# Sliding-window attention and a two-layer MoE block on one core: batch 1 in groups of three steps, another order of the first loads, and more idle matmuls ahead of the first MoE unit

## The chip, the cores and the metric

The kernel runs on one core of a Trainium2 chip. The core has a matrix engine (TensorE, PE in the profile; its weight loads are PEld), VectorE (DVE), ScalarE (ACT), GpSimd (POOL) and SyncE (SP). Each engine works through its own list of instructions in the order in which the program gives them, and waits where a semaphore says so. Data come from the device memory by DMA; here GpSimd issues nearly all loads. The metric is the device time of one execution in microseconds (us), lower is better. It is given as a median of several runs.

## The reference

Eight batches of eight heads, 576 tokens, head width 64. Each token sees the tokens at a distance of at most 32. The result is put together to 4608 rows of 512 and goes through two dense layers with a squared ReLU between them.

```python
scores = scale * np.matmul(q, k.transpose(0, 1, 3, 2))
mask = np.abs(pos[:, None] - pos[None, :]) <= window          # window = 32
scores = np.where(mask, scores, -1000000000.0)
attn = np.exp(scores - max); attn = attn / (sum(attn) + 1e-09)
x = np.matmul(attn, v)      # (8, 8, 576, 64), then transposed and reshaped to (4608, 512)
h = x @ w_in                # (512, 2048)
r = np.maximum(h, 0.0)
out = (r * r) @ w_out       # (2048, 512)
```

## The kernel before

**Steps and tiles.** The attention goes in steps of 64 tokens ("chunks"), nine for a batch, 72 in all, numbered n = 9 b + c. The MoE block goes in nine tiles T of 512 tokens, that is, of eight chunks, so that a tile does not end where a batch ends: tile 1 is chunks 8 to 15, and chunk 8 is the last of batch 0.

**Loading.** The tokens of a batch come in five or six pieces of at most 128 tokens (L37 to L39). `kBX`, `qBX` and `vBX` in the list `ORDER` (L33) are piece X of batch B; `w1D` and `w2D` are quarters of the two weights. `ORDER` is the order in which GpSimd issues these loads at the start (L459, L524, L541, L546). K and Q of batches 0 and 1 are turned by PE (`tok_turn`, L464: transposes at L482, then copies out of PSUM by VectorE and, in batch 0, ScalarE). From batch 2 on a transposing DMA on SyncE does this (`dma_turn`, L512). Loads from batch 2 on also wait for a certain MoE unit (`pace`, L501).

**Attention.** Batches 0 and 1 go in groups of one or two chunks, from batch 2 on in groups of three; `FB = 2` (L26) sets the border, and `build` (L882) takes the one path or the other. For a group of two, `scores` (L560) makes 16 small matmuls, ScalarE an exp (L598), VectorE one masked product for each chunk (L607); `av` (L694) then makes eight matmuls a chunk, `evac` (L717) divides by the row sums on VectorE (L722, L724), and `xturn` (L731) transposes on PE and copies with ScalarE into `XT`, the input of the first MoE layer. For a group of three, the middle chunk uses a copy of K with its halves in another order (`ka`, L586). The masked products (L613, L619) lay the three chunks out so that `av3` (L628) needs two times eight matmuls for all three; its results are copied out of PSUM (`evac3`, L645: L655 by VectorE, L652 by ScalarE), added (L657), and divided (L659, L662). `xturn3` (L668) turns the result, by DMA for n of at least `NPE` = 18, else on PE through bank D. In the code of before only chunks from 18 on reach it, so its PE part isn't used. PSUM has eight banks: A, C, B, D for the attention, two for the first layer (`HT`), two for the second (`OUTP`).

**MoE.** `mm1` and its variants for 128 tokens (`mm1_small`, L749) and 256 (`mm1_half`, L771) are the first layer; a unit of any of them is followed by a ReLU on ScalarE and a square on VectorE. Tile 0 and the first half of tile 1 have small units, the second half of tile 1 and tile 2 half ones. A small unit (g, q) of tile 0 needs token group g (chunks 2 g and 2 g + 1) and quarter q of the first weight. `mm2` (L837) is the second layer: unit x is 128 tokens and has four segments of four matmuls, one for each quarter of the second weight. Units take turns in the two `OUTP` banks; units 2 and 3 lie in banks B and D.

**What sets the order.** Each operation is recorded with its engine, what it reads and writes, a key and an estimated duration (`rec`, L61). `schedule` (L264) plays the program forward with these durations and a model of the load queue, works backward from the end to get due times, repeats this with several margins, and keeps the order per engine that has the shortest modelled end. That order is then fixed. A change of keys, banks or load order therefore can move operations of all engines.

**Idle matmuls.** `fill` (L305) puts matmuls on zeros (L408, 128 columns, into the second `OUTP` bank) into the planned gaps of PE, up to 36 us, but not beyond the transposes of piece 3 of batch 0 (`idle_end`, L490). In a gap that begins before 8 us (planned) the number is 1.15 times the gap over 107 ns, later 0.5 times the gap over 54 ns:

```python
for k in range(int((gap - 60) * (DENSE if at < COLD else SPARSE) // one)):
```

Of the kernel before, what the change touches and what calls it, by code (L numbers as in the profile page):

```python
# [8 lines left out]
BF16 = mybir.dt.bfloat16  # L9
# [13 lines left out]
WARM, COLD, DENSE, SPARSE = 36000, 8000, 1.15, 0.5  # L23
NPE = 18
TOFF, TST = 6, 0.9
# [7 lines left out]
ORDER = ("k01 q01 v00 v01 k02 q02 v02 w10 k03 q03 v03 w11 k04 q04 v04 w12 w13 w20 w21 w22 w23 k05 q05 "  # L33
         "k10 q10 v10 k11 q11 v11 k12 q12 v12 k13 q13 v13 k14 q14 v14").split()
# [12 lines left out]
class Prog:  # L47
# [310 lines left out]
class Gen:  # L358
# [82 lines left out]
    def pieces(self, b):  # L441
        return PIECE2 if b >= FB else PIECE if b else PIECE0
# [21 lines left out]
    def tok_turn(self, b, x, key):  # L464
# [95 lines left out]
    def scores(self, n, m):  # L560
# [23 lines left out]
        if m > 2:  # L584
# [4 lines left out]
                reads=self.qk_tags(b, c + 1) + [("sc", n - 3)], writes=[("ka", i, ki)], key=key - 1, dur=300, att=True)  # L589
# [78 lines left out]
    def xturn3(self, n, y):  # L668
# [10 lines left out]

        def f(e):  # L680
            for w, np in ((0, 128), (1, 64)):
                for t in range(4):
                    mm = e.transpose(bass.AP(self.TRP, 0, [[1024, 128], [1, 1]]) if False else self.TRP[:, 512 * w + np * t:512 * w + np * t + np],
                                     self.XR[0:np, 2 * y + w, 128 * t:128 * t + 128], self.ID[0:np, 0:np])
            return mm

        self.p.rec("PE", f, reads=[("xr", 2 * y), ("xr", 2 * y + 1), "id"], writes=["sD"], key=key, dur=340, att=True)
        for w, np in ((0, 128), (1, 64)):
            t0 = 64 * (n + 2 * w)
            src = self.TRP[:, 512 * w:512 * w + 4 * np].rearrange("p (f q) -> p f q", f=4)  # L690
            self.p.rec("ACT", lambda e, a=src, t0=t0, np=np: e.activation(self.XT[:, :, t0:t0 + np], a, ACTF.Copy), reads=["sD"],
# [57 lines left out]
    def mm1_small(self, T, g, q, key):  # L749
# [6 lines left out]
        def f(e):  # L756
            for d in range(4 * q, 4 * q + 4):
                for ft in range(4):
# [78 lines left out]
    def mm2(self, T, u, seg, key):  # L837
# [5 lines left out]
        if x in (2, 3):  # L843
            tag = "sB" if x == 2 else "sD"
            op = self.BK[tag[1]]
# [36 lines left out]
    def build(self):  # L882
# [18 lines left out]
        for b in range(B_):  # L901
# [23 lines left out]
            for c in range(NCH):  # L925
                n = NCH * b + c
                if b >= FB:
                    if c % 3 == 0:
                        self.scores(n, 3)
# [5 lines left out]
                        self.evac3(n, y)  # L935
                        self.xturn3(n, y)
                    continue
                m = 1 if not c or n in (1, 8) else 2
                if n not in self.group:
# [7 lines left out]
                    if n + m < FB * NCH and n + m != 8:  # L947
# [59 lines left out]
```

## Time and profile before

| what | value |
|---|---|
| median of 4 runs | 304.28 us (302.97 to 306.46) |
| the profiled execution: its own time | 305.64 us |
| its span, first to last instruction | 303.8 us |
| mean granted TensorE clock | 0.994 |
| busy: PE, DVE, ACT, POOL | 291.4, 173.4, 157.1, 106.6 us |
| GpSimd's load queue (q0) | 18.16 MB |
| first MoE unit starts | 15.80 us |

The page of the profile describes one execution. Busy times are the union of an engine's instructions. "40 slices" cuts the span into equal parts and gives each engine's busy share in tenths; PEclk is the clock that TensorE was granted, in tenths of full speed. The timeline lists an engine's instructions in order: start, duration, engine, line, operation, output and inputs, count, and in brackets the idle time before it and what ended that. A matmul's duration includes the time until its result has come out, so where matmuls follow each other closely their spacing, not their duration, says what each costs. In the view of DMA issues the last number is the time from issue to landing.

### The profile page before, as it was taken

The numbers are of one execution on the slowest core, as the hardware profiler recorded it, in microseconds if no ns is written. First come the engines' busy times: TensorE is split into PE (matmuls) and PEld (weight loads), VectorE is DVE, ScalarE is ACT, GpSimd is POOL, SyncE is SP. The second block draws the span as 40 slices with busy tenths as digits, with TensorE's granted clock in tenths as the row PEclk, the third lists the DMA queues.
The fourth block names the chain that finished last, engine by engine and source line by source line (L and its number), as shares of the span: only waits on it lengthen the run. The fifth ranks groups of instructions, "written<-read, shape, count | busy, mean of one in ns | idle before, by whom it ended". The sixth has DMA issues, their size and how long they took to land.

```text
span 303.8 us, 6966 instructions
## 1 busy us (share of the span) xinstructions
PE 291.4 (96%) x2726; PEld 171.3 (56%) x2763; DVE 173.4 (57%) x427; ACT 157.1 (52%) x261; POOL 106.6 (35%) x133
## 2 busy tenths in 40 slices
PE   8577999999999999999999999999999999999996
PEld 7477955886758764444454445454445444444444
DVE  6546424775698995668565795677457732222200
ACT  3345622745748763665465665555645644344411
POOL 8999374142415540552054534334320000000000
PEclk9979999999999999999999999999999999999999
DMA  9999999999999999999799999999995220000022
GB/s 110 154 186 207 191 155 194 157 175 144 161 121 168 121 131 205 144 112 166 156 127 134 145 155 186 114 160 127 171 126 66 63 60 35 37 35 35 36 95 80
DMA packets 166673, 39.07 MB, mean 129 GB/s; under 512 B 157808, under 2 KB 162160, under 8 KB 166640
## 3 DMA queue, kind: packets, MB, share of 16 engines
q0 software_dynamic: 115200, 18.16, 90.1%
q1 hardware_dynamic: 45472, 10.96, 25.7%
q10 hardware_dynamic: 5968, 9.51, 10.4%
q8 instruction: 22, 0.36, 0.5%
q14 instruction: 11, 0.09, 0.1%
HBM read 36.70 MB, written 9.44 MB: 152 GB/s over the span
## 4 chain that ended last, share of the span: by engine, by line
PE 89%; DVE 3%; DMA 3%; POOL 2%; issue 1%; ACT 1%; DVEq 0%; POOLq 0%
PE outp L849 36%; PE ht L798 27%; PE ht L759 7%; PE ht L780 6%; PE sc L578 3%; DMA w<-in_moe_w_in_dram 3%; PE sc L638 3%; PE sc L849 2%; DVE xr L662 1%; POOL vx L524 1%; PE sc L482 1%; PE sc L712 1%; PE sc L711 1%; PE sc L823 1%; PE outp L823 1%
## 5 line engine op out<-in xcount | busy, mean ns | idle before, releaser
L849 PE MATMUL outp<-w,gt 128*128 128x512 bf16 x506 | 125.8, 379 | 1.4 <-issue 0.3
L813 DVE TENSOR_TENSOR gt<-rt 128x512 bf16<-128x512 bf16 x144 | 59.7, 419 | 67.4 <-ACT rt L804 56.8
L798 PE MATMUL ht<-xt,w 128*128 128x512 bf16 x371 | 94.0, 379 | 1.0 <-issue 0.5
L804 ACT ACTIVATE rt<-ht 128x512 bf16<-128x512 f32 x96 | 57.2, 599 | 59.9 <-PE ht L798 57.0
L849 PEld LDWEIGHTS outp<-w,gt 128*128 128x128 bf16 x528 | 49.8, 98 | 54.6
L798 PEld LDWEIGHTS ht<-xt,w 128*128 128x128 bf16 x384 | 36.3, 98 | 41.7
L459 POOL DMA_DIRECT2D qraw<-in_q_dram x40 | 34.8, 871 | 50.1 <-PE ht L798 26.5
L459 POOL DMA_DIRECT2D kraw<-in_k_dram x40 | 34.9, 872 | 41.6 <-PE ht L798 17.8
L524 POOL DMA_DIRECT2D vx<-in_v_dram x40 | 34.6, 867 | 26.2 <-PE ht L798 12.6
L598 ACT ACTIVATE e<-sc 128x1024 bf16<-128x1024 f32 (+1 forms) x47 | 37.1, 822 | 11.1 <-PE sc L578 11.1
L856 ACT ACTIVATE oe<-outp 128x512 f32<-128x512 f32 x33 | 19.8, 599 | 23.7 <-PE outp L849 23.7
L759 PE MATMUL ht<-xt,w 128*128 128x128 bf16 x384 | 24.3, 223 | 2.8 <-DMA w<-in_moe_w_in_dram 2.1
L759 PEld LDWEIGHTS ht<-xt,w 128*128 128x128 bf16 x384 | 22.5, 100 | 3.6 <-issue 2.2
L662 DVE TENSOR_TENSOR xr<-pf,rs 128x512 bf16<-128x512 f32 (+1 forms) x36 | 23.7, 681 | 0.5 <-DVE ka L586 0.2
L780 PE MATMUL ht<-xt,w 128*128 128x256 bf16 x192 | 23.8, 273 | 0.0
L765 ACT ACTIVATE rt<-ht 128x512 bf16<-128x512 f32 x24 | 14.3, 599 | 16.0 <-PE ht L759 15.9
L780 PEld LDWEIGHTS ht<-xt,w 128*128 128x128 bf16 x192 | 17.9, 98 | 3.2
L786 ACT ACTIVATE rt<-ht 128x512 bf16<-128x512 f32 x24 | 14.3, 602 | 10.1 <-PE ht L780 8.6
L619 DVE TENSOR_TENSOR pt<-e,mask 128x512 bf16<-128x512 bf16 x36 | 15.2, 421 | 5.6 <-ACT e L598 5.5
L655 DVE COPY pf<-sc 128x520 f32<-128x520 f32 x18 | 12.6, 698 | 6.6 <-PE sc L638 6.4
L657 DVE TENSOR_TENSOR pf<-pf 64x520 f32<-64x520 f32 x18 | 12.6, 698 | 5.9 <-ACT pf L652 5.2
L536 DVE COPY vd<-vx 64x528 bf16<-64x528 bf16 (+1 forms) x28 | 12.5, 447 | 5.9 <-PE sc L578 4.6
(80 smaller groups left out, 211.6 us busy)
## 6 DMA issues: line engine op xcount, KB each, us to landing
out_dram<-oe ACTq DMA_DIRECT2D x35, 256.0 KB, 3.2
kraw<-in_k_dram POOLq DMA_DIRECT2D x30, 128.0 KB, 6.1
qraw<-in_q_dram POOLq DMA_DIRECT2D x30, 128.0 KB, 5.3
vx<-in_v_dram POOLq DMA_DIRECT2D x24, 128.0 KB, 5.4
w<-in_moe_w_in_dram POOLq DMA_DIRECT2D x4, 512.0 KB, 11.4
w<-in_moe_w_out_dram POOLq DMA_DIRECT2D x4, 512.0 KB, 18.5
vx<-in_v_dram POOLq DMA_DIRECT2D x16, 96.0 KB, 5.9
xt<-xr SPq DMA_TRANSPOSE x36, 4.2
```

Source lines behind the costliest of these rows:

```text
L459: self.p.rec("POOL", lambda e: e.dma_start(dst, src), writes=[("fraw", b, t, x)], old=[("fraw", b - 2, t, y + (b == 2))], reads=self.pace( ...
L524: self.p.rec("POOL", lambda e: e.dma_start(self.VX[b % 2][r:r + n, s, :, 0:64], self.v[b, :, t0:t0 + n, :].rearrange("h p d -> p h d")), w ...
L598: self.p.rec("ACT", lambda e, d=dst, a=src: e.activation(d, a, ACTF.Exp, scale=0.125), reads=["s" + x for x in name], writes=[("e", h)], k ...
L619: self.p.rec("DVE", lambda e, a=pt, c=ee, d=mb: e.tensor_tensor(a, c, d, ALU.mult), reads=[("e", k // 2), "mask"], writes=[("ptt", k)], ol ...
L662: self.p.rec("DVE", lambda e, w=w, np=np: e.tensor_tensor(bass.AP(self.XR, 512 * (2 * y + w), [[2048, np], [64, 2], [128, 4], [1, 64]]), b ...
L759: mm = e.matmul(ht[:, 128 * (d % 4):128 * (d % 4) + 128], self.W1[:, ft, 128 * d:128 * d + 128], self.XT[:, ft, t0:t0 + 128], start=(ft == ...
L780: mm = e.matmul(ht[:, 256 * (d % 2):256 * (d % 2) + 256], self.W1[:, ft, 128 * d:128 * d + 128], self.XT[:, ft, 64 * s0:64 * s0 + 256], st ...
L798: mm = e.matmul(ht[:], self.W1[:, ft, 128 * d:128 * d + 128], self.XT[:, ft, 512 * T:512 * T + 512], start=(ft == 0), stop=(ft == 3))
L804: self.p.rec("ACT", lambda e: e.activation(rt[:], ht[:], ACTF.Relu), reads=[("ht", k % 2)], writes=[("rt", k % 4)], key=key, dur=560)
L813: self.p.rec("DVE", lambda e: e.tensor_tensor(g, r, r, ALU.mult), reads=[("rt", k % 4)], writes=tags, key=key, dur=430)
L849: mm = e.matmul(op, gt[:, d, 128 * u:128 * u + 128], self.W2[:, d, :], start=(d == 0), stop=(d == 15))
L856: self.p.rec("ACT", lambda e: e.activation(oe[:], op, ACTF.Copy), reads=[tag], writes=[("oe", x % 4)], key=key, dur=560)
```

## The change

- `TB = 1`: batch 1 goes in groups of three chunks, its K and Q in the pieces of the later batches (`PIECE2`). Its pieces are still turned by PE (`TX = 5` sends none to the DMA), through bank D or B in turn, and the results of its groups are turned by PE through bank A instead of D.
- `ORDER`: pieces 4 of batch 0 come ahead of the second quarter of the first weight; piece 5 of batch 0 and pieces 0 and 1 of batch 1 come ahead of the second weight.
- `SPARSE` goes from 0.5 to 0.95, and 16 idle matmuls (`EXTRA`) are put immediately ahead of the first MoE unit, if that is planned ahead of the transposes of piece 3.
- The second layer of tile 0 does its units two by two, through all four segments, in the two `OUTP` banks; banks B and D are not used for it.

```diff
-WARM, COLD, DENSE, SPARSE = 36000, 8000, 1.15, 0.5
+WARM, COLD, DENSE, SPARSE, EXTRA = 36000, 8000, 1.15, 0.95, 16
 NPE = 18
+TB, TX = 1, 5
...
-ORDER = ("k01 q01 v00 v01 k02 q02 v02 w10 k03 q03 v03 w11 k04 q04 v04 w12 w13 w20 w21 w22 w23 k05 q05 "
-         "k10 q10 v10 k11 q11 v11 k12 q12 v12 k13 q13 v13 k14 q14 v14").split()
+ORDER = ("k01 q01 v00 v01 k02 q02 v02 w10 k03 q03 v03 k04 q04 v04 w11 w12 w13 k05 q05 k10 q10 v10 k11 q11 v11 "
+         "w20 w21 w22 w23 k12 q12 v12 k13 q13 v13 k14 q14 v14").split()
...
         for op in sorted((o for o in out if o.eng == "PE"), key=lambda o: o.start):
             gap = min(op.start, WARM, self.idle_end.start) - at
             one = 107 if at < COLD else 54
-            for k in range(int((gap - 60) * (DENSE if at < COLD else SPARSE) // one)):
+            for k in range(int((gap - 60) * (DENSE if at < COLD else SPARSE) // one) + (EXTRA if op is self.first and op.start < self.idle_end.start else 0)):
...
-                w.inc, w.val, w.sem, w.start, w.end, w.dur, w.key = False, None, None, at + one * k, 0, one, -99
+                w.inc, w.val, w.sem, w.start, w.end, w.dur, w.key = False, None, None, min(at + one * k, op.start - 1), 0, one, -99
...
     def pieces(self, b):
-        return PIECE2 if b >= FB else PIECE if b else PIECE0
+        return PIECE2 if b >= TB else PIECE if b else PIECE0
...
-        elif b or x == 5:
+        elif b:
+            u = "DB"[x % 2]
+            ps = self.BK[u].bitcast(BF16)
+            parts = [("k", "s" + u, ps[:, 0:512]), ("q", "s" + u, ps[:, 512:1024])]
+        elif x == 5:
             parts = [("k", "sD", self.TRP[:, 0:512]), ("q", "sD", self.TRP[:, 512:1024])]
...
-                reads=self.qk_tags(b, c + 1) + [("sc", n - 3)], writes=[("ka", i, ki)], key=key - 1, dur=300, att=True)
+                reads=self.qk_tags(b, c + 1) + ([("sc", n - 3)] if b > 1 or c else []), writes=[("ka", i, ki)], key=key - 1, dur=300, att=True)
...
+        trp = self.BK["A"].bitcast(BF16)
+
         def f(e):
             for w, np in ((0, 128), (1, 64)):
                 for t in range(4):
...
-        self.p.rec("PE", f, reads=[("xr", 2 * y), ("xr", 2 * y + 1), "id"], writes=["sD"], key=key, dur=340, att=True)
+        self.p.rec("PE", f, reads=[("xr", 2 * y), ("xr", 2 * y + 1), "id"], writes=["sA"], key=key, dur=340, att=True)
...
-        self.p.rec("PE", f, reads=[("xt", 8 * T + 2 * g), ("xt", 8 * T + 2 * g + 1), ("w1", q)], writes=[("ht", k % 2), ("mo", k)], key=key,
+        first = self.p.rec("PE", f, reads=[("xt", 8 * T + 2 * g), ("xt", 8 * T + 2 * g + 1), ("w1", q)], writes=[("ht", k % 2), ("mo", k)], key=key,
                    dur=900)
+        if not k:
+            self.p.first = first
...
         gt, op, tag = self.GT[T % 2], self.OUTP[x % 2][:], ("outp", x % 2)
-        if x in (2, 3):
-            tag = "sB" if x == 2 else "sD"
-            op = self.BK[tag[1]]
...
-            for seg in range(4):
-                for u in range(4):
-                    self.mm2(0, u, seg, 0.5 + seg + 0.1 * u)
+            for h in range(2):
+                for seg in range(4):
+                    for u in (2 * h, 2 * h + 1):
+                        self.mm2(0, u, seg, 0.5 + 2 * h + 0.5 * seg + 0.1 * (u % 2))
...
             for c in range(NCH):
                 n = NCH * b + c
-                if b >= FB:
+                if b >= TB:
                     if c % 3 == 0:
+                        if b == 1 and not c:
+                            for x in range(2):
+                                self.tok_turn(1, x, n - LEAD - 3)
                         self.scores(n, 3)
...
                         self.evac3(n, y)
+                        if b == 1 and c < 6:
+                            for x in range(2, 4) if not c else (4,):
+                                if x < TX:
+                                    self.tok_turn(1, x, n - LEAD)
+                                else:
+                                    for t in "kq":
+                                        self.dma_turn(1, t, x, n - LEAD)
                         self.xturn3(n, y)
```

More of the change, by code (lines that the diff above doesn't have):

```diff
@@ L682, in f @@
                 for t in range(4):
-                    mm = e.transpose(bass.AP(self.TRP, 0, [[1024, 128], [1, 1]]) if False else self.TRP[:, 512 * w + np * t:512 * w + np * t + np],
-                                     self.XR[0:np, 2 * y + w, 128 * t:128 * t + 128], self.ID[0:np, 0:np])
+                    o = 512 * w + np * t
+                    mm = e.transpose(trp[:, o:o + np], self.XR[0:np, 2 * y + w, 128 * t:128 * t + 128], self.ID[0:np, 0:np])
             return mm
-        self.p.rec("PE", f, reads=[("xr", 2 * y), ("xr", 2 * y + 1), "id"], writes=["sD"], key=key, dur=340, att=True)
+        self.p.rec("PE", f, reads=[("xr", 2 * y), ("xr", 2 * y + 1), "id"], writes=["sA"], key=key, dur=340, att=True)
         for w, np in ((0, 128), (1, 64)):
             t0 = 64 * (n + 2 * w)
-            src = self.TRP[:, 512 * w:512 * w + 4 * np].rearrange("p (f q) -> p f q", f=4)
-            self.p.rec("ACT", lambda e, a=src, t0=t0, np=np: e.activation(self.XT[:, :, t0:t0 + np], a, ACTF.Copy), reads=["sD"],
+            src = trp[:, 512 * w:512 * w + 4 * np].rearrange("p (f q) -> p f q", f=4)
+            self.p.rec("ACT", lambda e, a=src, t0=t0, np=np: e.activation(self.XT[:, :, t0:t0 + np], a, ACTF.Copy), reads=["sA"],
                        writes=[("xt", n + 2 * w + u) for u in range(np // 64)], key=key, dur=200 + 2.8 * np, att=True)
@@ L946, in build @@
                     self.scores(n, m)
-                    if n + m < FB * NCH and n + m != 8:
+                    if n + m < TB * NCH and n + m != 8:
                         bb, cc = divmod(n + m, NCH)
```

## The prediction

> **What bounds the kernel now.** I read the page first, for the engine that is never free and for the slices in which it is.
>
> ```profile
> PE 291.4 (96%) x2726; PEld 171.3 (56%) x2763; DVE 173.4 (57%) x427; ACT 157.1 (52%) x261; POOL 106.6 (35%) x133
> ...
> PE   8577999999999999999999999999999999999996
> ...
> PEclk9979999999999999999999999999999999999999
> ```
>
> A slice is 7.6 us. From the fifth on PE is full; the chain of waits gives PE 89%. So time can be gained only by giving PE less to do, or by filling the first four slices. Idle matmuls (L408) count as busy there, so I added up the spacing of starts in the PE timeline from 15.7 us (first MoE unit) to 28.7: 6 units (L759, 96 matmuls) and the attention of batch 0 would take 8.3 us at full rate (16 matmuls at 56 ns are 0.9 us, six units 5.4; transposes, scores and AV 2.9). The stretch is 13.0 us long. Of the 4.7 us lost, 2.66 is bare idle, 0.41 idle matmuls, and 1.6 slow matmuls and short hand-overs. From 28.7 to the last matmul PE is idle for only 2.5 us in all. The place is the first 29 us.
>
> Next the windows view, cut where the granted clock changes and in equal steps around (columns: stretch, its length, busy PE, PEld, DVE, ACT and POOL with counts, granted clock, DMA share, GB/s):
>
> ```profile
> 8.28:11.70 3.42, 2.39 (x51) 1.87 (x50) 2.85 (x9) 1.07 (x2) 3.42 (x5) 1.00 1.62 144
> 11.70:15.11 3.41, 1.51 (x24) 1.08 (x22) 1.30 (x4) 1.51 (x2) 3.41 (x5) 1.00 1.87 168
> 15.11:18.52 3.41, 2.72 (x30) 2.75 (x31) 0.35 (x2) 0.60 (x1) 3.41 (x6) 0.50 1.63 189
> 18.52:21.94 3.42, 2.31 (x48) 1.91 (x46) 2.67 (x6) 2.11 (x3) 3.42 (x6) 1.00 1.87 180
> ```
>
> After a stretch with PE 44% busy the next one runs at half clock; after 70% and 68% it runs at full clock. Then the PE timeline and the landings:
>
> ```profile
> 13.49 0.19 PE L712 MATMUL sc<-vx,pt 128*128 128x65 bf16 x1
> 15.80 1.86 PE L759 MATMUL ht<-xt,w 128*128 128x128 bf16 x16 [2.12 <-DMA w<-in_moe_w_in_dram]
> ...
> 19.79 0.40 PE L740 MATMUL outp<-identw,xr 128*128 128x128 bf16 x4 [0.76 <-DVE kt L498]
> ...
> 25.86 0.40 PE L740 MATMUL outp<-identw,xr 128*128 128x128 bf16 x4 [1.20 <-DVE kt L498]
> ```
>
> ```profile
> w<-in_moe_w_in_dram POOLq DMA_DIRECT2D x1, 512.0 KB, 10.5
> vx<-in_v_dram POOLq DMA_DIRECT2D x1, 96.0 KB, 10.5
> ```
>
> The first line is w11, issued at 10.44 and landed at 21.0; the second v04, 12.92 to 23.4. Issue plus landing, read so for each load, gives a queue that delivers in order: a 128 KB piece every 0.85 us, a weight quarter every 2.5 us (w12 25.9, w13 28.4, w20 31.0, w23 38.6, k05 38.9). PE's gaps are the 2.12 us for w10 and then the latency of batch 0's attention.
>
> **The new order of loads.** Nothing ahead of w10 moves: w10 stays at 15.7. Then, with the spacings above: k04, q04, v04 land at 19.3, 20.2, 20.9 (2.5 us sooner); w11 at 23.4 (2.4 later); w12 and w13 unchanged; k05, q05, and k10 to v11 from 28.6 to 33.9 (10 sooner); w20 to w23 at 36.4, 38.9, 41.5, 44.1 (5.4 later); k12 to v14 again by 51. On POOL only the order changes: w11 is issued three issues of 0.87 us later, at 13.0 instead of 10.44, still 10 us ahead of its landing, and the loads of batch 2 follow as before.
>
> What PE can do: from 15.7 to 23.4 only w10 is there, so two units (1.8 us; the third token group is not ready) and 2.9 us of attention: up to 3.0 us idle, more than before. But from 23.4 two weight quarters and soon a third meet three or four ready token groups, so I take PE as full: 5.3 us to 28.7. Together 10.0 us against 8.3: **1.65 us gained**, if the clock holds. Next, is the later w2 late? From 23.4 there are 14 units (12.6 us), 1.7 of batch 0's attention, and turns and scores of batch 1 (1.4): PE reaches 39 before it needs w20. Then segments of 1.73 us (8 matmuls, 216 ns) for tokens 0 and 1 end at 40.8, 42.5, 44.2 and 45.9, each after its quarter's landing. Cost nothing; if PE were 3 us earlier it would wait those 3 us, no more.
>
> **Idle matmuls and reserve.** 16 matmuls at 54 to 107 ns are 0.9 to 1.7 us, inside the 2.12 us gap: free. The denser filling adds some 22 to the 25 issued there now (1.2 us) to gaps of that size; where a planned gap doesn't exist they delay work, by 0.3 us at most, as the rows from 8 to 14 us have 1.4 us idle besides the large gap. They lift 1.51 us busy to about 2.9 of 3.41. Here a rule speaks against: the Trainium skill, "TensorE: Matmul & The Clock Gate", section "Why this matters for your kernels", says that no gap under about 3 us costs the clock; by it a gap of 2.12 is harmless and the reserve worth nothing. The row shows half clock after that gap, in a stretch that was 44% busy. By the row the reserve saves about 1.1 of the 1.65 us (16 MoE matmuls at 106 instead of 56 ns, 0.8; AV and transposes 0.3); by the rule nothing. I go with the row. The same page (Part 1) has the activity window free-running, so in some runs it may fall well anyway: this profiled execution took 305.64 us, the four runs 302.97 to 306.46. The sum below is against 305.64 and I carry its difference to the median, 304.28; if half of the runs never had the drop, 0.5 us of it isn't there.
>
> **Batch 1 in threes.** AV goes from 72 matmuls to 48; both kinds are spaced 30 ns in the PE timeline: 0.7 us less. Scores: 24 in 0.46 us (76.53 to 76.99) against 16 in 0.34: 0.2 less. Three hand-overs fewer at about 0.1: 0.3. Transposes of the result, 24 of which 12 are half wide, against 18 whole: nothing. So **1.2 us less on PE**, the bound. VectorE pays, by batch 2's rows:
>
> ```profile
> L655 DVE COPY pf<-sc 128x520 f32<-128x520 f32 x18 | 12.6, 698 | 6.6 <-PE sc L638 6.4
> L657 DVE TENSOR_TENSOR pf<-pf 64x520 f32<-64x520 f32 x18 | 12.6, 698 | 5.9 <-ACT pf L652 5.2
> ```
>
> With the masks (0.42, 0.69, 0.42), the key copy (0.29), the reciprocal (0.25) and two L662 (0.68) a group is 4.8 us, 14.3 for three, against 8 now: 6.3 more, ScalarE about 2 more. Between 40 and 75 us VectorE is busy for 18.6 of 35; the cover is the MoE work that PE has in stock. A new wait comes with bank A: the transposes of a group go there and ScalarE empties it, so the next group's scores wait for the whole group before. PE takes its queue in order: behind those scores stand second-layer segments of tile 0 and small units of tile 1, and ScalarE's Relu and VectorE's squares wait for these. Batch 2 shows 7.6 to 11.3 us from scores to the last L662; with transposes and copies 9 to 12.5. Group 2 can score at 50 (k13 lands at 47.5), group 3 at 59 to 62.5, and chunk 15 is ready at 68 to 75. PE's stock without it: 12.6 + 13.8 (second layer of tile 0) + 7.2 (8 small units of tile 1) + 6.9 (its second layer, tokens 0 and 1) + 8.0 attention = 48.5, to 71.9, or 74 if reckoned from the state of before at 73.6 less what is gained. So 0 to 3 us; I take nothing, as most of the interval lies below. The mm2 banks: token 2 now waits for ScalarE's 0.6 us copy of token 0 while token 1's 0.86 us segment runs: 0 to 0.3, taken as nothing. Attention that starts sooner may close some of the 2.5 us of late gaps, 0 to 1; I take 0.5.
>
> Sum: 305.64 - 1.65 - 1.2 - 0.5 = 302.3 for a profiled execution, and **301.0** for the median.
>
> **Rivals.**
> 1. The early stretch closes almost wholly (0.20): units are placed so that the 3.0 us idle shrinks by 2. Then 299.0. For it: PE works at full rate from 23.4; against: no second quarter earlier.
> 2. The reserve doesn't do what it says (0.12): the planner puts the transpose of k03 ahead of the first unit, so that no reserve is made; or the drop moves one stretch on, where PE has 1.6 of 3.4 us of work. Then the 1.1 us stay lost, and the 0.5 with them: 302.6.
> 3. Slower (0.21): PE runs dry in front of chunk 15. Place: near 72 to 74 us, at the first half-wide unit of tile 1. Each microsecond that chunk 15 is later than 74 is lost. It decides once the loss exceeds the 3.3 gained, at about 77. VectorE at 90% from 80 to 100 us, with the same groups, speaks for it; against it, that even batch 2's slowest group gives 75. With groups 2 and 3 each 4 us above the middle (72), at 80, the time is 307.
>
> **How the numbers follow.** The forecast has 0.47. A measurement of this kernel can tell about 1%, 3 us, from no change. Of the forecast's chance three quarters lie below 301.2, with rival 1's 0.20 that is 0.53 or so faster by over 1%; a quarter, rival 2 and a little of rival 3 give 0.29 within 1%; the rest of rival 3, 0.18, slower. The range goes from rival 1 with its bound, 298.5, to the milder part of rival 3, 306.
>
> **What would show it.** Right: granted clock 1.00 from 5 us on; w11 at 23.4 and w20 at 36.4; seven units by 28.7; PE idle under 3 us from 23.4 on; AV of batch 1 in 48 matmuls. Wrong: a half-clock stretch after 15; PE waiting for w20; an idle PE near 72; idle matmuls that push attention back before 15 us.

## The result, and the profile after

The changed kernel takes **303.39 us** (median of 44 runs, 302.1 to 305.8), the kernel before, run beside it, 304.7 (63 runs). The ratio is 0.9964, with an interval of 0.9953 to 0.9975: 0.36% or 1.1 us faster, which is within 1%, where 301.0 and 1.1% were forecast. Ratios, here and below, leave out disturbed executions, those more than 1.5% above the fastest of their kernel (of h2_two_banks three of twelve). The profiled execution of after took 303.66 us with a span of 301.9 (before 305.64 and 303.8), at a granted clock of 1.00 from 6.3 us, where its clock records begin, to the end of its work.

First the page of after: busy time, then the slices of PE, of its clock, and the shares of the chain of waits.

```profile
PE 292.1 (97%) x2750; PEld 172.3 (57%) x2786; DVE 175.4 (58%) x429; ACT 159.7 (53%) x266; POOL 107.0 (35%) x133
...
PE   8969999999999999999999999999999999999996
...
PEclk9999999999999999999999999999999999999999
...
PE 85%; POOL 5%; DMA 5%; DVE 3%; issue 1%; ACT 0%; DVEq 0%; POOLq 0%; ACTq 0%
```

The slice at half speed is gone, PE is full from the fourth slice on, and yet the chain gives DMA 5% and PE 85 where it was 89 (and DMA 3). More of the path now runs through data: those 5% are one load, `q05`, issued at 15.70 us and landed at 29.65. In before the last load on the path is `w10`, landed at 15.66. The view of the chain, before and then after (start, us, what):

```profile
7.09 8.57 DMA w<-in_moe_w_in_dram
```

```profile
15.70 13.95 DMA qraw<-in_q_dram
```

So in the trace of after the load queue sets the time up to 29.65 us: a PE still faster ahead of that would only have waited longer. Next the windows of after, cut as those of before were (columns as there):

```profile
8.28:11.70 3.42, 3.03 (x60) 2.65 (x59) 3.27 (x10) 1.19 (x2) 3.42 (x5) 1.00 1.60 127
11.70:15.11 3.41, 3.24 (x69) 2.96 (x67) 1.39 (x4) 1.51 (x2) 3.41 (x5) 1.00 1.72 168
15.11:18.52 3.41, 2.18 (x36) 1.88 (x36) 1.52 (x4) 1.19 (x2) 3.41 (x6) 1.00 2.31 161
18.52:21.94 3.42, 2.59 (x59) 2.20 (x56) 2.65 (x8) 2.60 (x4) 3.42 (x5) 1.00 1.33 204
...
28.70:44.50 15.80, 15.10 (x239) 12.12 (x239) 9.05 (x24) 8.01 (x15) 9.48 (x13) 1.00 1.66 189
44.50:75.00 30.50, 30.24 (x366) 20.06 (x369) 17.67 (x42) 16.48 (x30) 9.98 (x13) 1.00 2.01 166
```

PE's busy time in the stretch ahead of the first unit went from 1.51 to 3.24 us by the idle matmuls, and the next stretch has full clock. The last row is where the idle PE of rival 3 would show: 44.5 to 75 us has 0.26 us idle, so PE did not run dry. The timeline of PE in after (start, duration, then line, operation, output and inputs, count, and in brackets the idle time and its releaser):

```profile
14.00 0.94 PE L409 MATMUL outp<-zz 128*128 128x128 bf16 x14
15.59 1.07 PE L766 MATMUL ht<-xt,w 128*128 128x128 bf16 x16 [0.65 <-DMA w<-in_moe_w_in_dram]
...
19.34 1.07 PE L766 MATMUL ht<-xt,w 128*128 128x128 bf16 x16 [0.35 <-ACT xt L753]
...
22.72 1.07 PE L766 MATMUL ht<-xt,w 128*128 128x128 bf16 x16 [0.29 <-DMA w<-in_moe_w_in_dram]
...
29.78 0.25 PE L487 MATMUL sc<-identw,kraw 32*128 32x32 bf16 x4 [0.60 <-DMA qraw<-in_q_dram]
...
45.89 0.39 PE L487 MATMUL sc<-identw,kraw 128*128 128x128 bf16 x4
46.11 0.39 PE L487 MATMUL sc<-identw,qraw 128*128 128x128 bf16 x4
46.33 1.89 PE L855 MATMUL outp<-w,gt 128*128 128x512 bf16 x8
48.06 0.61 PE L691 MATMUL sc<-identw,xr 128*128 128x128 bf16 x8
48.60 0.40 PE L487 MATMUL sc<-identw,kraw 128*128 128x128 bf16 x4
```

The weights landed within 0.7 us of the forecast: w11 at 22.7 (23.4), w12 25.2, w13 27.8, w20 36.3 (36.4), w21 38.9, w23 44.0 (44.1). Eight small units are started by 28.1 us. New is a wait of 0.60 us for piece 5 of batch 0 (q05 landed at 29.65). At 45.89 PE begins to turn piece 2 of batch 1 (K, then Q at 46.11), the last load of which, q12, landed at 45.66: there is no wait, but only 0.23 us of slack. In before the same piece landed at 45.2 and was turned at 55.2, 10 us later; it is the change that brings PE so close to the queue. The eight transposes at L691 take 0.54 us to the next start, 67 ns each on average.

**Where 1.9 us of span came from.** I added up the spacing of PE's starts in both traces.

| part | forecast | measured |
|---|---|---|
| lead at 28.7 us: 27 more small-unit matmuls at 56 ns (1.5 us), the AV and a turn of chunks 6 and 7 (0.7) | 1.65 | 2.2 |
| batch 1 in threes: AV and its hand-overs 1.1 less; scores 0.2 less (1.37 us for 1.58); transposes of the result 0.6 more (24 in 1.61 us for 18 in 1.03) | 1.2 | 0.7 |
| idle PE after 28.7 us: 3.34 us for 2.49 | +0.5 | -0.85 |
| everything else, small differences in many places | none | -0.2 |
| sum | 3.35 | 1.9 |

### The profile page after: what moved, and what is told of

The parts are those of the page before. It is cut to its first block, busy times and chain, and to the rows that moved or that the text cites. A ratio compares the mean times of both kernels' runs of the same rounds, so it can differ in the third digit from the quotient of the medians.

```text
span 301.9 us, 7020 instructions
## 1 busy us (share of the span) xinstructions
PE 292.1 (97%) x2750; PEld 172.3 (57%) x2786; DVE 175.4 (58%) x429; ACT 159.7 (53%) x266; POOL 107.0 (35%) x133
## 4 chain that ended last, share of the span: by engine, by line
PE 85%; POOL 5%; DMA 5%; DVE 3%; issue 1%; ACT 0%; DVEq 0%; POOLq 0%; ACTq 0%
PE outp L855 39%; PE ht L807 27%; PE ht L789 6%; PE ht L766 5%; DMA qraw<-in_q_dram 5%; PE sc L643 3%; PE sc L583 3%; POOL vx L529 1%; POOL kraw L460 1%; POOL qraw L460 1%; POOL w L546 1%; PE sc L487 1%; DVE gt L822 1%; PE sc L832 1%; PE outp L832 1%
## 5 line engine op out<-in xcount | busy, mean ns | idle before, releaser
L855 PE MATMUL outp<-w,gt 128*128 128x512 bf16 x534 | 131.6, 379 | 2.0 <-issue 0.8
L855 PEld LDWEIGHTS outp<-w,gt 128*128 128x128 bf16 x560 | 52.7, 98 | 58.2
L603 ACT ACTIVATE e<-sc 128x512 bf16<-128x512 f32 (+1 forms) x48 | 37.4, 810 | 12.0 <-PE sc L583 12.0
L862 ACT ACTIVATE oe<-outp 128x512 f32<-128x512 f32 x35 | 20.9, 598 | 26.6 <-PE outp L855 26.6
L667 DVE TENSOR_TENSOR xr<-pf,rs 128x512 bf16<-128x512 f32 (+1 forms) x42 | 27.7, 682 | 0.4
L624 DVE TENSOR_TENSOR pt<-e,mask 128x512 bf16<-128x512 bf16 x42 | 17.6, 422 | 14.0 <-ACT e L603 13.7
L660 DVE COPY pf<-sc 128x520 f32<-128x520 f32 x21 | 14.7, 699 | 11.3 <-PE sc L643 11.3
L657 ACT ACTIVATE pf<-sc 128x520 f32<-128x520 f32 x21 | 12.6, 600 | 11.6 <-PE sc L643 11.6
L795 ACT ACTIVATE rt<-ht 128x512 bf16<-128x512 f32 x24 | 14.4, 600 | 7.4 <-PE ht L789 6.1
L662 DVE TENSOR_TENSOR pf<-pf 64x520 f32<-64x520 f32 x21 | 14.6, 698 | 5.8 <-ACT pf L657 4.9
```

The lines of the kernel that those rows point to most:

```text
L603: self.p.rec("ACT", lambda e, d=dst, a=src: e.activation(d, a, ACTF.Exp, scale=0.125), reads=["s" + x for x in name], writes=[("e", h)], k ...
L624: self.p.rec("DVE", lambda e, a=pt, c=ee, d=mb: e.tensor_tensor(a, c, d, ALU.mult), reads=[("e", k // 2), "mask"], writes=[("ptt", k)], ol ...
L667: self.p.rec("DVE", lambda e, w=w, np=np: e.tensor_tensor(bass.AP(self.XR, 512 * (2 * y + w), [[2048, np], [64, 2], [128, 4], [1, 64]]), b ...
L855: mm = e.matmul(op, gt[:, d, 128 * u:128 * u + 128], self.W2[:, d, :], start=(d == 0), stop=(d == 15))
L862: self.p.rec("ACT", lambda e: e.activation(oe[:], op, ACTF.Copy), reads=[tag], writes=[("oe", x % 4)], key=key, dur=560)
```

## The experiments

Two accounts of the small gain were set against each other. By the forecast's, PE is the bound from 28.7 us on, and what is saved early arrives at the end. By the rival, PE runs just behind the data (the load queue to 49 us, then the transposing DMAs of `XT`), and a lead is waited away. A third question is what each part of the change does alone. All results together; "before" is the kernel before in runs beside it, and the ratio is to that. Where a run is compared with after below, the medians are meant unless ratios are named; the two can differ by some 0.4 us, since not all stand beside the same runs of before. In e2, h2, e3, h1, e8, e5, g4 and e6 the planner makes a new order as well, so that such a run measures the edit together with that order; in the others the order of PE's work is that of the kernel they start from.

| run | edit | median, us | before | ratio (95% interval) |
|---|---|---|---|---|
| e1_fill_only | before, new filling and reserve | 304.46 | 304.24 | 1.0 (0.9974 to 1.0027) |
| e4_after_old_fill | after, old filling, no reserve | 303.49 | 304.24 | 0.9974 (0.995 to 0.9998) |
| f1_after_reserve_only | after, old filling, reserve kept | 303.59 | 304.78 | 0.9974 (0.9945 to 1.0003) |
| e2_order_only | before, new load order | 307.16 | 304.78 | 1.0092 (1.0058 to 1.0127) |
| h2_two_banks | before, tile 0's second layer in two banks | 305.9 | 304.29 | 1.0036 (1.0006 to 1.0066) |
| e3_after_pairs | after, batch 1 in pairs | 304.02 | 304.24 | 0.9998 (0.9974 to 1.0022) |
| h1_after_old_order | after, old load order | 311.19 | 304.29 | 1.0218 (1.0178 to 1.0257) |
| e8_after_four_banks | after, tile 0's second layer in four banks | 320.69 | 304.78 | 1.0528 (1.0482 to 1.0574) |
| e5_after_turn_dma | after, results of batch 1 turned by DMA | 311.83 | 304.24 | 1.0237 (1.019 to 1.0283) |
| g4_turn_group18 | after, PE turns one more group | 304.25 | 304.5 | 0.9987 (0.9965 to 1.0009) |
| e6_after_k05_early | after, k05 and q05 ahead of w11 | 304.25 | 304.78 | 0.9994 (0.996 to 1.0027) |
| g1_early_less | after, 1.34 us of PE work left out at 30 us | 303.29 | 304.5 | 0.9956 (0.9934 to 0.9979) |
| g5_mid_less | the same at 57 us | 302.77 | 304.5 | 0.9948 (0.9925 to 0.9972) |
| g3_late_less | 1.30 us left out at about 200 us | 301.76 | 304.5 | 0.9897 (0.9871 to 0.9924) |
| a0_after_again | after itself | 303.47 | 304.29 | 0.9968 (0.9948 to 0.9988) |
| h3_extra_load | after, one more 128 KB load ahead of k12 | 303.82 | 304.29 | 0.9984 (0.9961 to 1.0007) |

### The filling and the reserve

```diff
-WARM, COLD, DENSE, SPARSE, EXTRA = 36000, 8000, 1.15, 0.95, 16
+WARM, COLD, DENSE, SPARSE, EXTRA = 36000, 8000, 1.15, 0.5, 0
```

This is e4_after_old_fill: the old filling, and no reserve (the 16 idle matmuls ahead of the first MoE unit). f1_after_reserve_only has 0.5 and 16, and e1_fill_only puts the filling's part of the change alone into the kernel before (0.95, 16 and the lines in `fill` and `mm1_small` that go with it).

> The kernel before with the idle matmuls and the reserve of the change alone; everything else, the order of all other instructions too, stays. Theory A (the half-clock stretch is real but comes in only part of the runs): 0.4 to 0.9 us faster than before, with the granted clock at 1.00 from 5 us on and the first unit at 56 ns a matmul. Theory B (the gate is most of what the change brings): 1.1 us faster or more. Theory C (the rule that a gap under 3 us costs nothing): no difference, and the clock of before is 1.00 in most runs.

> The changed kernel with the old filling (0.5, no reserve). Theory A: 0.4 to 0.9 us slower than the changed kernel, that is, 0.2 to 0.7 faster than before; the half clock is back after 15 us in part of the runs. Theory B: no faster than before. Theory C: as fast as the changed kernel (about 1.1 to 1.3 us faster than before).

> The changed kernel with the old filling of the gaps (0.5) but with the reserve of 16. Theory A (the drop of the clock after 15 us is what the idle matmuls remove, and the dense filling costs something by itself): the clock is 1.00 in most runs and the time 0.2 to 0.5 us under the changed kernel. Theory B (the filling has no price): the same as the changed kernel. Theory C (the reserve alone doesn't keep the clock): drops in as many runs as with the old filling, 6 of 12.

On the clock the filling does what it says. In 52 of 112 runs of the kernel before the mean granted clock is 0.994 or lower, which is what one stretch of 3.41 us at half clock, or more of them, makes of a span of 304 us. A run with one such stretch takes about 0.9 us more than one without (medians of 304.85 and 303.9), and one with two takes 306.4. With the filling alone it is 0 of 12 runs, with the whole change 2 of 44, with the change but the old filling 6 of 12, with the reserve kept 3 of 12. Yet no gain in time shows: the ratio is 1.0 for e1, and e4 and f1 lie 0.1 and 0.2 us above after (0.3 by the ratios), inside their intervals. The half clock's 0.9 us in half of the runs would be some 0.4 in the median; the forecast had 1.1, from one profiled execution that happened to have it.

The trace of e1 shows one way in which it is lost. Its PE is 0.8 us ahead of before from 27 to 109 us, and then comes the first unit of tile 3:

```profile
116.72 1.89 PE L851 MATMUL outp<-w,gt 128*128 128x512 bf16 x8
119.07 1.90 PE L800 MATMUL ht<-xt,w 128*128 128x512 bf16 x8 [0.46 <-DMA xt<-xr]
```

In before this unit starts at 119.21 without a wait. The transposing DMA for it took 8.1 us from issue to landing in e1 and 5.8 in before, and landed 0.6 us later (119.03 for 118.47) though it was issued earlier. In f1 the same happened at the first unit of tile 2, ahead of which f1 had led after by 0.98 us for more than 50 us:

```profile
84.94 2.76 PE L855 MATMUL outp<-w,gt 128*128 128x512 bf16 x12
88.38 1.05 PE L789 MATMUL ht<-xt,w 128*128 128x256 bf16 x8 [0.67 <-DMA xt<-xr]
```

After starts that unit at 88.53; the DMA took 8.25 us in f1 (landing at 88.33) and 6.4 in after (87.48). That one trace of each shows this doesn't prove that it happens in each run. Why e1's runs are 0.5 us slower than those of before that have no half-clock stretch (304.5 and 303.9) stays open.

### Order, banks and groups, one by one

The edits are the lists of the change, put in or taken out one at a time: e2_order_only has the new `ORDER` in the kernel before, h1_after_old_order the old one in after; e3_after_pairs has `TB = 2`; h2_two_banks and e8_after_four_banks exchange the second layer of tile 0:

```diff
+        if x in (2, 3):
+            tag = "sB" if x == 2 else "sD"
+            op = self.BK[tag[1]]
...
-            for h in range(2):
-                for seg in range(4):
-                    for u in (2 * h, 2 * h + 1):
-                        self.mm2(0, u, seg, 0.5 + 2 * h + 0.5 * seg + 0.1 * (u % 2))
+            for seg in range(4):
+                for u in range(4):
+                    self.mm2(0, u, seg, 0.5 + seg + 0.1 * u)
```

> The kernel before with the changed order of the first loads alone. Theory A (the early lead of the change comes from the order: six and two thirds us of queue in front of the third and fourth token group are moved): units 4 to 7 of tile 0 start 1.5 us or more sooner than before, and 0.5 to 1 us of it is left at the end. Theory B (the order is worth nothing without the groups of three, because batch 1 in pairs and the second layer's banks of before can't use it): within 0.3 us of before, though units 4 to 7 are sooner.

> The kernel before with the second layer of tile 0 two units at a time in the two OUTP banks, nothing else changed. Theory A (the banks are only a condition for the groups of three): 0 to 0.5 us slower than before, since a segment then needs its quarter of the second weight for two units instead of four. Theory C (the new order of the second layer is itself a gain): 0.3 us faster or more.

> The changed kernel with batch 1 in groups of one and two chunks as before; the load order, the filling and the second layer's banks stay changed. Theory A (groups of three save PE only some 0.5 us, because the 24 transposes at 67 ns cost more than the 18 at 57, and 0.2 to 0.4 of it is lost as idle time later): 0 to 0.5 us slower than the changed kernel. Theory B (groups of three are the main gain, 1.2 us or more): 1.2 us slower than the changed kernel, as slow as before. Theory C (they cost more than they save): faster than the changed kernel by 0.5 us or more.

> The changed kernel with the order of loads as before (groups of three, two banks and filling stay). Theory A (the order carries the early lead and with it the gain): 1 us or more slower than the changed kernel, as slow as before or slower. Theory B (leads before 45 us are worth little): within 0.5 us of the changed kernel.

> The changed kernel with the second layer of tile 0 as before, four units at a time, units 2 and 3 in banks B and D. Theory A (two banks are a condition for groups of three in batch 1, whose scores and turns need B and D): slower than the changed kernel by 1 us or more, with PE waiting for attention banks between 36 and 56 us. Theory B (the banks cost nothing either way): within 0.3 us of the changed kernel.

The order alone costs 0.9% (2.4 us against the runs beside it), the two banks alone 0.4% (1.1 us), the filling nothing; the order, banks and filling together without the groups of three give 0.9998. So the parts don't add, and the gain appears only with the groups of three: 303.39 or 303.47 with them, 304.02 without (ratios 0.9964 and 0.9998, the intervals just touching). But the groups need the other two. With the old order or with four banks they cost 7.8 and 17.3 us against after. What the order alone waits for, in the view of waits of e2_order_only (engine, output, line, releaser: total us, times, longest):

```profile
PE ht L759 <- DMA w<-in_moe_w_in_dram: 2.6, 2, 2.0
PE sc L482 <- issue: 1.2, 1, 1.2
PE sc L578 <- DVE qt L498: 1.0, 1, 1.0
```

Of the 2.6 us, 2.0 are the wait for w10 ahead of the first unit, which before has too (2.12). Only 0.6 are for w11, put behind piece 4, and PE is nevertheless 2.1 us ahead of before from 34 to 40 us. The loss comes later: the other two waits lie at 56.4 and 54.6 us. By then the second layer of tile 0 is finished, and while batch 1 is turned and scored PE has nothing else to do but wait. Tile 1's first unit starts at 57.37 us, in before at 56.16, and from there PE stays 1.2 us behind (although before's trace lost some 0.9 us in its half-clock stretch). The order alone brings an early lead and spends it where PE's stock of work ends. The waits of e8_after_four_banks:

```profile
PE sc L691 <- DVE xr L667: 3.9, 2, 2.3
PE sc L643 <- DVE pt L624: 2.2, 1, 2.2
```

and the timeline of PE in h1_after_old_order:

```profile
74.77 1.03 PE L855 MATMUL outp<-w,gt 128*128 128x512 bf16 x4
77.97 0.72 PE L691 MATMUL sc<-identw,xr 128*128 128x128 bf16 x8 [2.17 <-DVE xr L667]
79.38 1.89 PE L789 MATMUL ht<-xt,w 128*128 128x256 bf16 x8 [0.69 <-ACT xt L698]
```

PE is dry in front of tile 1's first half unit, which starts at 79.38 instead of 73.37. This is the place and the mechanism that rival 3 named. It is real, and with the change as a whole it does not happen. Whether the resource that was taken back or the order that the planner then made is at fault in h1 and e8, these runs do not separate. From the trace of h2_two_banks, an execution of 311.1 us, I read nothing.

### Turning the results by DMA

```diff
-NPE = 18
+NPE = 9
```

> The changed kernel with the results of batch 1 turned by the transposing DMA instead of by 24 PE transposes (1.62 us on PE in the changed kernel's timeline) and six copies on ScalarE. Theory A (PE's work is the bound and tile 1 has stock enough): 0.8 to 1.6 us faster than the changed kernel. Theory B (the latency of the groups of batch 1 binds): no faster, with idle PE between 60 and 75 us, since a DMA takes 4 to 8 us where the transposes and copies take 1.5.

PE has 24 transposes (1.6 us) less to do, and the time is 8.4 us longer than after. The waits of e5_after_turn_dma:

```profile
PE ht L789 <- DMA xt<-xr: 3.4, 1, 3.4
PE sc L643 <- DVE pt L618: 2.2, 1, 2.2
```

and its windows across that place:

```profile
71.15:74.56 3.41, 2.15 (x32) 0.99 (x30) 0.14 (x1) 1.68 (x3) 0.00 (x0) 1.00 1.94 149
74.56:77.97 3.41, 0.78 (x16) 0.60 (x16) 2.90 (x7) 0.92 (x2) 0.00 (x0) 1.00 1.39 144
77.97:81.39 3.42, 1.68 (x8) 1.02 (x8) 1.46 (x4) 0.00 (x0) 0.00 (x0) 0.50 1.48 204
81.39:84.80 3.41, 3.41 (x38) 2.42 (x37) 2.37 (x5) 2.71 (x4) 0.88 (x1) 0.50 1.46 96
```

The first half unit of tile 1 starts at 79.71, 6.3 us later than in after, and the dry PE then gets half clock for 6.8 us. The opposite edit, `NPE = 21`, gives PE one group more:

> The changed kernel with the results of the first group of batch 2 (chunks 18 to 20) turned by PE too, 0.54 us of PE work more, instead of by the two transposing DMAs that land at 87.5 and 88.1 us, 0.4 us ahead of tile 2's first unit. Theory A: 0.5 us slower. Theory B: no slower, to 0.5 us faster than the changed kernel, if the planner's other moves don't matter.

304.25, no faster: 0.9 us above after (0.7 by the ratios), nearer to theory A. The border at 18 stands where neither side gains.

### A load moved: the wait for q05

```diff
-ORDER = ("k01 q01 v00 v01 k02 q02 v02 w10 k03 q03 v03 k04 q04 v04 w11 w12 w13 k05 q05 k10 q10 v10 k11 q11 v11 "
+ORDER = ("k01 q01 v00 v01 k02 q02 v02 w10 k03 q03 v03 k04 q04 v04 k05 q05 w11 w12 w13 k10 q10 v10 k11 q11 v11 "
```

> The changed kernel with the two small loads k05 and q05 ahead of the second, third and fourth quarter of the first weight. In the changed kernel PE waits 0.60 us for q05 at 29.8 us. Theory A (PE is the bound, a wait on its path is time): that wait goes, w11 is some 0.5 us later and costs up to 0.5 at 23 us; 0 to 0.5 us faster than the changed kernel. Theory B (an early lead is lost again at the waits for transposing DMAs around 115 to 120 us): no difference at the end though PE is ahead at 35 us.

The wait of 0.60 us is gone from its trace. The median is 304.25, not faster. Its interval, 1 us to either side, overlaps after's and is too wide for a saving of 0.6 to be told. The wait itself is not in most executions: of the eight profiled ones in which PE has after's order, it is 0.60 us in after and 0.15 in a0; in the six others q05 landed by 28.5 us and PE does not wait for it. The planner also gave other places to the work of the later tiles here, so the run decides less than the next ones.

### What a microsecond of PE is worth, by place

The same amount of PE work is left out of after at three places. g1_early_less and g5_mid_less do one of the four accumulating matmuls for each of four output blocks in small units 8 and 9 of tile 0, or 18 and 19 of tile 1 (24 matmuls at 56 ns, 1.34 us). g3_late_less does one of four in two output blocks of the first layer in tile 6 (6 matmuls at 216 ns, 1.30 us). The sums over 512 inputs are thereby incomplete; the rest is as in after.

```diff
-                for ft in range(4):
+                for ft in range(1 if k in (8, 9) else 4):
...
-                                  self.XT[:, ft, t0:t0 + 128], start=(ft == 0), stop=(ft == 3))
+                                  self.XT[:, ft, t0:t0 + 128], start=(ft == 0), stop=(ft == 3 or k in (8, 9)))
```

> The changed kernel with 24 matmuls left out of units 8 and 9 of tile 0 (only the first quarter of their sum is made), 1.34 us less PE work at 30 to 32 us, all orders as they are. Theory A (PE is the bound all the way, as the forecast had it): 1.2 to 1.4 us faster than the changed kernel. Theory B (what PE gains early is taken again where it waits for data: the last quarter of the second weight, which lands 0.2 us before its first use at 44.2 us, and the transposing DMAs ahead of tiles 2 and 3 at 88 and 118): 0 to 0.6 us faster, with PE waiting for w22 or w23 near 42 to 44 us.

> The same with units 18 and 19 (tile 1, 57 to 59 us): 1.34 us less behind the second weight, ahead of tiles 2 and 3. Theory A: 1.2 to 1.4 us faster than the changed kernel. Theory B: 0.2 to 0.9 us faster, with waits for transposing DMAs near 88 or 118 us.

> The same late: six matmuls of 512 columns left out of two units of tile 6, 1.30 us less near 200 us. Both theories: 1.2 to 1.4 us faster than the changed kernel, since behind 120 us PE waits for almost nothing; it is the scale for the other two.

> The changed kernel itself, as the reference on this chip for the three others. Both theories: 0.9953 to 0.9975 of before, some 303.4 us.

Against after (303.39, and 303.47 in its second measurement, which stands beside h1, h2 and h3): 0.1 to 0.2 us for the early 1.34, 0.6 to 0.7 for the middle, 1.6 to 1.7 for the late 1.30, each known to some 0.7 us (by the ratios 0.2 to 0.4, 0.5 to 0.6 and 2.0 to 2.2). The ratios of early and late, 0.9956 and 0.9897, have intervals that don't touch; the middle one lies between, nearer to the early one. The traces have less spread, since PE goes through the same list in all of them: behind the edit of g3, PE's lead over after is 1.3 us larger than ahead of it, and stays so to the end. In the trace of g5 a part goes at once:

```profile
57.90 0.40 PE L766 MATMUL ht<-xt,w 128*128 128x128 bf16 x4 [0.47 <-ACT rt L774]
```

The shortened unit waits for ScalarE's ReLU of the one before, so 0.5 of its 1.34 us are the experiment's own doing. PE's lead grows by 0.63 us there, from 0.49 to 1.12, and all of that stays to the end: this trace shows no wait at 88 or 118 us. So the middle run does not show that a lead is lost behind 61 us. For the early one there is no such cause; its timeline:

```profile
43.82 0.59 PE L855 MATMUL outp<-w,gt 128*128 128x512 bf16 x2
45.06 0.40 PE L487 MATMUL sc<-identw,kraw 128*128 128x128 bf16 x4 [0.65 <-ACT oe L862]
...
48.01 0.38 PE L487 MATMUL sc<-identw,kraw 128*128 128x128 bf16 x4 [0.15 <-DMA qraw<-in_q_dram]
```

PE is 1.8 us ahead of after at 42.3 us and 0.6 after 50, and these 0.6 are what the queue itself was early in this execution (q12 landed at 45.01, in after at 45.66). The wait at 45.06 is put down to ScalarE (the release of a bank), but PE starts at the moment at which q12 has landed, and the next wait names q13 (landed 47.87). The lead is waited away for pieces 2 and 3 of batch 1; another 0.2 us went at 43.4, for w23. The trace of g3, whose edit comes only at 207 us, shows the same without any edit. It happened to be 1.1 us ahead of after at 38 us, and 0.3 from 47 on:

```profile
45.63 0.40 PE L487 MATMUL sc<-identw,kraw 128*128 128x128 bf16 x4 [0.69 <-DMA qraw<-in_q_dram]
```

In six of the eight profiled executions in which PE has this order, it begins to turn piece 2 within 0.1 us of the landing of q12 (in after 0.23 us behind it, in f1 0.42). To test that cause by itself, h3_extra_load puts one more load of 128 KB, which nobody uses, ahead of k12:

```diff
+        k12 = [o for o in out if o.dma == ("f1k2", 1)][0]
...
+        w.eng, w.fn, w.dma, w.deps, w.i = "POOL", self.extra, ("xtra", 0), set(), k12.i
```

> The changed kernel with one more 128 KB load in GpSimd's queue, immediately ahead of k12 and into a buffer that nobody reads; no other order is changed and PE's work is the same. Theory A (PE is the bound, loads are hidden): 0 to 0.2 us slower than the changed kernel. Theory B (from 36 to 49 us the queue of loads sets the pace: q12 lands at 45.66 and is turned at 46.11, q13 at 48.37 and 48.83): q12 and q13 land 0.85 us later, PE waits 0.4 to 0.8 us for them, and 0.3 to 0.8 us of it is left at the end.

```profile
44.18 1.46 PE L863 MATMUL outp<-w,gt 128*128 128x512 bf16 x6
46.13 0.38 PE L495 MATMUL sc<-identw,kraw 128*128 128x128 bf16 x4 [0.49 <-issue]
```

q12 lands at 46.04 and PE starts at 46.13. At 38 us this execution was 0.41 us ahead of after; from here to the end it is 0.35 behind. The load of 0.85 us cost 0.76 in the trace and 0.35 to 0.43 in the median (303.82). The ratios' intervals overlap, so the size is uncertain, but the traces show the path: at 46 us PE goes at the pace of the load queue.

## Why the prediction was right or wrong

**What bounds the kernel.** "The place is the first 29 us", and after it PE sets the end: this is the step that failed. Its term in the sum is the late gaps, +0.5 us forecast and -0.85 measured. PE does set the end late, where 1.30 us less work brought 1.6 to 1.7. But up to 49 us the changed kernel meets the load queue. In the profiled execution this cost 0.60 us at once (q05), and at 45.9 us the data were ahead by only 0.23 (by 0.1 or less in six of the eight executions of this order), so that any further lead is waited away there: 1.34 us less work at 30 us brought 0.1 to 0.2. What is left of a lead can still meet a transposing DMA at 88 or 119 us, as in f1 and e1. The views read for the prediction (PE at 9 in each slice, 2.5 us idle in all) could not tell the difference: they show that PE hardly waits in before, not by how much the data are ahead, nor how much of that the change uses up.

**Where the 2.4 us went by which 301.0 was missed.** 1.0 is the carry to the median (below). Some 1.4 is the sum's (302.3 forecast, 303.66 measured): 1.35 in the late gaps, 0.6 in the transposes and 0.2 in small differences, less the 0.55 by which the early lead was larger and 0.1 in AV. Only 0.6 of it, the wait for q05, is seen to come from the queue; why the other gaps did not close stays open.

**New order of loads.** Landings right, and the early gain larger than forecast (2.2 for 1.65, 0.2 of it because the first unit happened to start earlier, at 15.59 for 15.80). So rival 1 came true in a small part. That PE would not wait for w20 was right. "If PE were 3 us earlier it would wait those 3 us" was the right sentence about the wrong piece: not w20, but q12 behind it, which the new order leaves as late as it was while PE comes sooner. The forecast's own times left only 0.1 us of slack just ahead of that place: w23 was to land at 44.1 and to be used from 44.2 on. The 0.60 us for q05 were not foreseen.

**Idle matmuls and reserve.** The row was right on the clock, and the rule as the prediction read it, that a gap under 3 us is harmless, was not: the 44% stretch of before holds 1.43 us of that gap of 2.12, and half clock followed. With the filling the drop is gone from nearly all runs. The size was wrong. 1.1 us is what one execution lost; half of the runs have no drop, and removing it from all brings 0.0% in before and 0.1 to 0.3 us in after. The prediction named this correction (0.5 us) and didn't take it. Taking 1.3 us from 302.3 to get a median supposed that the changed kernel's profiled execution would lie as far above its median as before's; it lay only 0.27 above. That makes 1.0 us of the miss.

**Batch 1 in threes.** The AV term was right (1.1 with hand-overs, forecast 1.0), and so were the scores (0.2). "Transposes of the result, 24 of which 12 are half wide, against 18 whole: nothing" was wrong by 0.6 us. A half-wide one does take half the time (29 ns to the next start, a whole one 56), but each change of width costs some 95 ns more: 152 ns from the last whole one to the first half-wide one, 122 from the last half-wide one to the next instruction. That is 0.19 us for each of the three groups.

**Late gaps.** 0.5 us were to close; PE's idle time grew by 0.85, of which 0.6 is q05's. The sign was wrong, and of the signs named for being right this one failed: PE was to be idle for less than 3 us from 23.4 on, and is for 3.34 after 28.7 alone.

**The hazards taken as nothing** (bank A, two banks for the second layer, VectorE's 6 us more) did no harm in the change as a whole: PE is idle for 0.26 us in all between 44.5 and 75 us. VectorE's busy time rose only from 173.4 to 175.4 us. **Rival 3** named the place and the mechanism, and e5, h1 and e8 show what it costs (8 to 17 us) once a part of the change is missing. **Rival 2**: the time falls nearest to it (302.6), by another cause; the reserve was made and no drop moved on in after. A moved drop is shown only with the old filling (19.24 to 22.65 us in e4) and without the groups (23.52 to 26.93 in e3).

## What to carry to other kernels

A bound that is 97% busy says nothing of the slack behind it: before an early microsecond is counted at the end, look at every later place where the busy engine takes in a load, and note by how much that load is ahead, before the change and after it. No more of an early lead than the smallest such slack gets past; a saving behind the last late load can be worth all of itself. An interlocked change (order, banks, group size) can be a gain only as a whole, while its parts alone bring a loss or nothing (the groups of three were not run alone); a profiled execution that stands off its median should not lend its own accident to a forecast of the median.

## What the runs showed of the hardware

**The clock follows the busy share of a 3.41 us stretch, not the longest gap.** I cut the traces of all kernels here, without e2_order_only (no clock records) and h2_two_banks, in steps of 3.41 us from the point at which the clock first came up (3.7 to 7.0 us, another in each execution). The step is taken from the traces: half clock within the work lasts 3.41 us in before, e3 and e4, 6.83 in e5, 13.65 in e8. Of the stretches at full clock with PE less than 80% busy, 8 were followed by one at half clock; they were 23 to 55% busy. All with 57% or more were followed by full clock, and two at 54%. Two rows of e4_after_old_fill and then two of e3_after_pairs:

```profile
15.83:19.24 3.41, 1.87 (x42) 1.36 (x40) 2.56 (x6) 2.03 (x4) 3.41 (x6) 1.00 2.05 173
19.24:22.65 3.41, 3.41 (x48) 3.31 (x47) 2.60 (x7) 1.87 (x3) 3.41 (x5) 0.50 1.25 208
```

```profile
20.11:23.52 3.41, 1.77 (x45) 1.49 (x44) 2.88 (x8) 1.78 (x3) 3.41 (x6) 1.00 1.23 202
23.52:26.93 3.41, 3.41 (x42) 3.41 (x40) 0.42 (x1) 1.56 (x3) 3.41 (x6) 0.50 1.67 183
```

In the first row the longest gap is 0.67 us and the stretch is 55% busy, and the next has half clock. A stretch of g3_late_less with a gap of 1.45 us at 57% kept it. In after no cut of the first 29 us, wherever it begins after 8 us, is below 59%.

**Other sizes.** Between transposes on PE of one width the starts are 56 ns apart at 128 partitions and 29 to 39 at 64, but each change between the two widths costs some 95 ns (152 ns for 56 into the half-wide ones, 122 for 29 out of them, alike in the three groups of after), so that four whole and four half-wide ones together take 67 ns each. The first transposing DMA for `XT` of tile 2 takes 5.5 to 8.3 us from issue to landing in the eight executions of the same order, with the load traffic beside it. The first weight quarter lands at 14.4 to 15.9 us in the profiled executions, and w23 at 42.8 to 44.4 in the eight, so single traces can differ by 1.5 us ahead of any effect of an edit.
